# Attention's projections as two 64-row lanes from rows with halves exchanged, and the maxima transposed behind the values

## The chip, the cores and the metric

The program runs on one core of one Trainium2 chip. The metric is the device time of one execution in microseconds (us), the median over runs. TensorE (PE) multiplies matrices from SBUF into PSUM banks, and its weight loads (PEld) are listed apart. VectorE (DVE), ScalarE (ACT) and GpSimd (POOL) work on SBUF and PSUM, and SyncE (SP) starts the DMAs. Each engine takes its instructions in program order.

## The reference

Four layers follow one another on an array x of 2048 rows and 640 columns: spectral, attention, spectral, attention. Each adds its result to x.

```
x = x + A(layernorm(x));  x = x + B(layernorm(x));  x = x + A(layernorm(x));  x = x + B(layernorm(x))
A: y = Cr @ (x @ Wr.T) - Ci @ (x @ Wi.T)            # Fourier mixing over columns, then over rows
B: q, k, v = split(x @ wqkv)                         # 32 heads of 20 columns
   scores = q @ k.T / sqrt(20); a row sees itself and the 255 rows ahead of it
   o = softmax(scores) @ v;  y = o @ wo
```

## The kernel before

Each product of f32 data is made of f16 parts: both factors are split into a high and a low part, and three of the four combinations are added up. A product over 640 columns is thus 15 matmuls of 128 rows each (five pieces of 128 columns, three combinations) into one PSUM bank. Such products in attention are q and k ("qk": 128 columns of weights as the stationary side, 256 rows of x streamed, QB = 256), v (320 columns of weights streamed) and out (320 columns streamed, HD = 320). All matmuls and transposes go through one helper, `tensor` (L116), which also fixes their order on PE to the order in which the code is written.

Attention (`attention`) goes through 8 blocks of 256 rows, and each block takes 32 steps `g`, one for each pair of query tile and heads, 256 steps in a layer and some more for the work that lags behind. A step does, in this order on PE:

- `scores(g)`: four matmuls into tile sp, each on 64 of the array's 128 rows (62 used), two heads side by side. DVE then masks (L1054) and takes the maximum of each row (m, L1058).
- `by_key(g - KEY_LAG)`: six matmuls into tile tp, the same scores turned so that keys lie in rows, again 64-row tiles. ACT makes the softmax weights from them, ptq (L1102), and POOL applies masks. There is one tile tp of two banks, so the next step's tp waits until ACT has read this one.
- every fourth step `values`: 32 f32 matmuls into tile pv, in four column tiles of 32. ACT copies the result to pvs (L1135), and `back` (two steps later) turns it back and divides.
- every fourth step `hand_on`: the maxima of four steps (tile tops) are transposed on PE into a bank of pool p3, and ACT copies them into two rows of the query tile (qs, L1079, `copy_tops`), where by_key's matmuls subtract them. HAND_LAG = 4 puts the transposes at the end of a step, and the two copies come one and two steps later.
- `run_fill`: the projections of the next block, out products of the block before, and turns (transposes of rows for them) fill PE in between. A list `fill` holds them as units that become ready at some step and have a due step. Each step gets a budget of PE time, `rate`, times a factor from the table FILL, which has one number for each of the four steps of a period.

Each unit of a product runs to its end in one of the two banks of pool pf, its result is taken out by ACT (qf L334, v L824) or DVE (x L879), and a turn uses the single bank of pool p3. The copies that take a turn out of PSUM are L952 (DVE) and L954 (ACT). The results q and k go to DRAM and come back as stacks by heads, 160 KB a DMA. `last_out` makes the out products of the last block piece by piece, as heads become ready; L852 adds them to x and SP writes 160 KB each time.

In PSUM lie then: pf two banks, sp two, tp two, pv one, p3 one. SP issues all DMAs (L174).

Of the kernel before, what the change touches and what calls it, by code (L numbers as in the profile page):

```python
# [11 lines left out]
F32 = mybir.dt.float32  # L12
# [17 lines left out]
NST = 5  # L30
EARLY = 4 * ND * P + NST * 2 * QB
# [3 lines left out]
FILL = (1.3, 1.12, 0.28, 1.3)  # L35
# [7 lines left out]
HAND_LAG = 4  # L43
# [7 lines left out]
TURN_ROOM = 1000  # L51
NORM_STEPS = (4, 9)
# [10 lines left out]
def body(ctx: ExitStack, tc: tile.TileContext, x_in, cmat, whid, wqkv, wo, out):  # L63
# [3 lines left out]
    pf_ = ctx.enter_context(tc.tile_pool(name="pf", bufs=1, space=bass.MemoryType.PSUM))  # L67
# [42 lines left out]
    in_turn, latest = [False], [None]  # L110
# [74 lines left out]
    def new_f():  # L185
        return pf_.tile([P, 512], F32, tag="f", name="pf", bufs=2)

# [12 lines left out]
    B11, T2, B21, T3, T1, T4, B22 = range(7)  # L200

    class Hidden:
# [21 lines left out]
        def stage(self, s, pool, new=new_f):  # L224

            w, xt = self.w, self.xt(s)
            if s % 8 < 2:
                zc = new_early()[:, :14 * HD].rearrange("p (m a d) -> p m a d", m=7, a=2)
            else:
                zc = pool.tile([P, 7, 2, HD], F16, tag="zc", name="zc", bufs=4)  # L230
            self.zc[s] = zc
            b11, b12, t1, t2, t3, t4 = (self.zf[:, k] for k in range(6))
            z = None

            def product(c, n):
                nonlocal z
                z = new()
                cs = slice(n * HD, (n + 1) * HD)
                k = 0
                for dt in range(ND):  # L240
                    for l, r in ((0, 0), (0, 1), (1, 0)):
                        self.last = matmul(z[:, :HD], xt[:, l, dt], w[:, r, c, dt, cs],
                                                     start=k == 0, stop=k == 14).ins
                        k += 1
                        yield 136
                z = z[:, :HD]
# [11 lines left out]
            yield from product(0, 0)  # L258
            scaled(zc[:, B11, 0])
            scaled(b11)  # L260
            minus(zc[:, B11, 1], zc[:, B11, 0])
            yield 0
            yield from product(0, 1)
            scaled(b12)
            minus(t1, b11)
            parts(T1, t1)
            yield 0
            yield from product(1, 1)
            scaled(zc[:, B22, 0])
            minus(t2, t1)  # L270
            minus(t3, b12)
            minus(zc[:, B22, 1], zc[:, B22, 0])
            parts(T2, t2)
            parts(T3, t3)
            yield 0
            yield from product(1, 0)
            scaled(zc[:, B21, 0])
            minus(zc[:, B21, 1], zc[:, B21, 0])
            minus(t4, t2)
            parts(T4, t4)  # L280
            yield 0

    def new_stack():
        return new_quad("ks").bitcast(F16).rearrange("p (a b) -> p a b", a=NP)

# [13 lines left out]
    class Projections:  # L299


        def __init__(self):
            n = 3 * ND * D
            big = new_big()
            self.w = [big[:, k * n:(k + 1) * n].rearrange("p (a b) -> p a b", a=ND) for k in range(2)]
            load_behind([(big[:, k * n:(k + 1) * n], bw_d[k].rearrange("p a b -> p (a b)")) for k in range(2)])
            self.rows = {}
            self.turn = 0
            self.stack = {}

        def new_rows(self, b):
            t = new_early()
            n = 2 * ND * P
            x = t[:, :2 * n].rearrange("p (t a b c) -> p t a b c", t=2, a=2, b=ND)
            st = t[:, 2 * n:].rearrange("p (m a t) -> p m a t", m=NST, a=2)
            self.rows[b] = (x, [st[:, k] for k in range(NST)])

        def qk(self, b, w, ct):
            pf = new_f()
            cols = slice(w * D + ct * P, w * D + (ct + 1) * P)  # L320
            xt, stores = self.rows[b]
            k = 0
            for dt in range(ND):
                for l, r in ((0, 0), (0, 1), (1, 0)):
                    matmul(pf[:, :QB], self.w[l][:, dt, cols], xt[:, :, r, dt, :],
                                     start=k == 0, stop=k == 14)
                    k += 1
                    if k < 15:
                        yield 109
            t = stores[self.turn % len(stores)]  # L330
            self.turn += 1
# [6 lines left out]
            yield 109  # L338
# [5 lines left out]
    def spectral(layer, res_src, hidden, first):  # L344
        with ExitStack() as st:
# [6 lines left out]
            sb = pool("sb")  # L352
            pxy = banks("px")
            w = hidden.w
# [210 lines left out]
            def ahead(proj):  # L565
# [3 lines left out]
                for w in (1, 0):  # L569
                    for ct in range(ND):  # L570
                        for _ in proj.qk(0, w, ct):
                            pass
                        yield 1
# [3 lines left out]
            def finish(j, pace):  # L577
# [15 lines left out]
                for k, xs in enumerate(xss):  # L593
                    for m in range(2):
                        transposed(xs, m, proj.rows[j][0][:, k])
                        yield 1
                    finished[0] += 1
# [168 lines left out]
    def attention(layer, proj, dst, final):  # L766
        with ExitStack() as st:
# [6 lines left out]
            sb = pool("sb")  # L774
            if layer == 0:
# [6 lines left out]

            def new_turn():

                return p3.tile([P, 512], F32, tag="f", name="pt") if in_turn[0] else new_f()
# [15 lines left out]
            def proj_qk(b, w, ct):  # L801
                yield from proj.qk(b, w, ct)
# [3 lines left out]
            def proj_v(b, ti, n):  # L806
                j = 2 * b + ti
                if n == 0:
# [4 lines left out]
                pf = new_f()  # L813
                cols = slice(2 * D + n * 320, 2 * D + (n + 1) * 320)
                k = 0
                for dt in range(ND):
                    for l, r in ((0, 0), (0, 1), (1, 0)):
                        matmul(pf[:, :320], proj.rows[b][0][:, ti, l, dt, :], proj.w[r][:, dt, cols],
                                         start=k == 0, stop=k == 14)
                        k += 1  # L820
                        if k < 15:
                            yield 136
# [3 lines left out]
                yield 136  # L826

            def out_turn(i, k):
                if k == 0:
                    X2[i] = keep.tile([P, D], F32, tag="res", name="x3", bufs=4)  # L830
                    load(X2[i], x2_d[i])
                    OT[i] = sb.tile([P, 2, ND, P], F16, tag="ot", name="ot", bufs=2)
                yield from turned(OS[i // 2][:, :, i % 2], k, OT[i])
                done.add((i, k))

            def last_out(i, d0, d1):

                if d0 == 0:
                    x3 = keep.tile([P, D], F32, tag="res", name="x3", bufs=4)
                    load(x3, x2_d[i])  # L840
                    OT[i] = (sb.tile([P, 2, ND, P], F16, tag="ot", name="ot", bufs=2),
                             ps.tile([P, 2, 512], F32, tag="ts"[i % 2 == 0], name="acc"), x3)
                ot, acc, x3 = OT[i]
                for k in range(2):
                    yield from turned(OS[i // 2][:, :, i % 2], k, ot, d0, d1)
                for n in range(2):
                    yield from out_products(ot, acc[:, n], n, d0, d1)
# [7 lines left out]
                if not final:  # L855
                    yield from next_layer(i, x3)

            def out_products(ot, o, n, d0, d1):
                cs = slice(n * 320, (n + 1) * 320)
                for dt in range(d0, d1):  # L860
# [441 lines left out]
```

## Time and profile before

| | |
|---|---|
| time, median of 3 runs | 2274.68 us (2274.08 to 2276.71) |
| the profiled execution: its time, its span, its granted clock | 2273.16 us, 2271.4 us, 0.987 |
| attention's steps, first layer | about 600 to 1152 us of the span |
| attention's steps, second layer | about 1717 to 2240 us of the span |
| DMA | 292.94 MB, mean 129 GB/s, 254 in the busiest of 40 slices |

The span is the time between the first and the last record of the profile, and the profiled execution's own time is 1.8 us longer. In the profile's rows a start and a duration stand first. The duration of a matmul includes its latency, so what a matmul costs in a stream is read from start to start. "Waits" list idle time of an engine and what ended it; "the chain" is the work that ended last, followed back.

### The profile page before, as it was taken

What the parts mean: (1) busy time and instruction counts of PE and PEld (TensorE: products, weight loads), DVE (VectorE), ACT (ScalarE), POOL (GpSimd) and SP (SyncE); (2) the same over time, 40 slices, a digit from 0 to 9 for tenths busy, and PEclk for the clock granted to TensorE, in tenths of its full rate; (3) what the DMA queues carried; (4) which work ended last, traced back from release to release, by engine and by line L of the source; (5) the groups of instructions that cost most, each with busy time, mean ns of one, the idle gap of its engine ahead of it and who ended that gap; (6) DMA issues with size and microseconds to landing.
All of it is one profiled execution on the core that took longest, in us unless ns stands there. A gap on an engine that the chain in (4) does not pass through costs nothing.

```text
span 2271.4 us, 55086 instructions
## 1 busy us (share of the span) xinstructions
PE 2132.5 (94%) x21985; PEld 1498.7 (66%) x21985; DVE 1632.5 (72%) x3577; ACT 1291.8 (57%) x2159; POOL 1387.0 (61%) x1788
## 2 busy tenths in 40 slices
PE   7989889899899999999898999999998999999997
PEld 4757666667666666677555777777676666777664
DVE  7886758866678787886756858585757777777664
ACT  6434455443367777777754443433434777777775
POOL 5775868857355665565445858586674545566443
PEclk9999999999999999999999999999999999999999
DMA  7664646454532322333324536363643323332231
GB/s 247 214 214 136 211 162 213 162 194 165 138 83 68 94 75 72 92 90 86 129 76 142 195 130 207 112 207 137 254 125 97 81 57 83 93 95 56 56 76 36
DMA packets 187605, 292.94 MB, mean 129 GB/s; under 512 B 13908, under 2 KB 120660, under 8 KB 178004
## 3 DMA queue, kind: packets, MB, share of 16 engines
q1 hardware_dynamic: 187348, 289.43, 40.9%
q8 instruction: 172, 2.82, 0.5%
q14 instruction: 85, 0.70, 0.1%
HBM read 202.51 MB, written 86.87 MB: 127 GB/s over the span
## 4 chain that ended last, share of the span: by engine, by line
PE 61%; DVE 14%; issue 5%; POOL 4%; ACT 3%; DMA 2%; SPq 0%; DVEq 0%; POOLq 0%; ACTq 0%
PE pf L116 25%; PE pv L116 8%; PE y L116 8%; PE z L116 5%; PE x L116 5%; PE sp L116 5%; DVE m L1058 3%; DVE sp L1054 3%; PE tp L116 3%; PE pt L116 2%; DVE cc L488 2%; ACT ptq L1102 1%; DMA x<-x2d 1%; DVE lnt L141 1%; PE acc L116 1%
## 5 line engine op out<-in xcount | busy, mean ns | idle before, releaser
L116 PEld LDWEIGHTS <-cc 128*128 128x128 f16 x5376 | 526.7, 98 | 220.6 <-issue 17.6
L1102 ACT ACTIVATE ptq<-tp,shift,alpha 128x768 f32<-128x768 f32 (+2 forms) x512 | 486.7, 951 | 176.1 <-PE tp L116 166.0
L116 PEld LDWEIGHTS <-big 128*128 128x128 f16 x4320 | 410.6, 99 | 148.7 <-issue 34.0
L1058 DVE TENSOR_REDUCE m<-sp 128x2 f32<-128x512 f32 (+1 forms) x512 | 344.9, 674 | 16.7
L1054 DVE COPY_PREDICATED sp<-mask,sp 128x256 f32<-128x256 int32 x448 | 191.0, 426 | 203.0 <-PE sp L116 186.7
L1107 POOL TENSOR_SCALAR_AFFINE_SELECT ptq<-ptq 128x512 f32<-128x512 f32 x224 | 145.4, 649 | 261.2 <-ACT ptq L1102 260.5
L116 PE MATMUL pf<-early,big 128*128 128x256 f16 x2400 | 304.5, 273 | 0.0
L485 ACT ACTIVATE cc<-cs 128x512 f16<-128x512 f32 x256 | 151.6, 623 | 241.3 <-POOL cs L478 119.2
L116 PE MATMUL y<-zc,cc 128*128 128x320 f16 x1728 | 266.3, 301 | 6.4 <-DVE pf L511 6.1
L488 DVE SCALAR_TENSOR_TENSOR cc<-cs,cc 128x512 f16<-128x512 f32 x256 | 252.2, 1000 | 13.2 <-ACT cc L485 12.9
L116 PE MATMUL pf<-big 128*128 128x320 f16 x1680 | 243.7, 304 | 17.2 <-DVE zc L256 8.3
L488 DVE SCALAR_TENSOR_TENSOR cc<-cq,cc 128x512 f16<-128x512 f32 x192 | 192.2, 1002 | 0.1
L1109 POOL TENSOR_SCALAR_AFFINE_SELECT ptq<-ptq 128x512 f32<-128x512 f32 x256 | 164.1, 641 | 43.7 <-ACT ptq L1102 43.7
L116 PE MATMUL pv<-ptq,v 128*32 128x128 f32 (+1 forms) x3840 | 183.8, 331 | 0.0
L116 PE MATMUL z<-zc,cc 128*128 128x320 f16 x1152 | 179.7, 301 | 3.7 <-DVE res L511 3.7
L116 PE MATMUL x<-zc,cc 128*128 128x320 f16 x1152 | 180.2, 301 | 0.0
L116 PE MATMUL sp<-ks,qs 62*128 62x256 f16 (+1 forms) x1792 | 154.3, 249 | 17.2 <-DVE m L1058 15.1
L1079 ACT ACTIVATE qs<-pt 2x512 f16<-2x512 f16 x224 | 131.4, 586 | 47.8 <-PE pt L116 45.2
L116 PE MATMUL pf<-big,early 128*128 128x320 f16 x960 | 157.6, 300 | 0.8 <-DVE x L879 0.8
L116 PE MATMUL tp<-qs,ks 62*128 62x128 f16 x2688 | 150.6, 217 | 4.4 <-ACT ptq L1102 3.4
L116 PE MATMUL pf<-bo,ot 128*128 128x320 f16 x840 | 141.9, 302 | 6.1 <-DVE ot L952 6.1
L116 PEld LDWEIGHTS <-ks 62*128 62x128 f16 x3008 | 116.5, 94 | 43.3 <-DVE m L1058 20.1
(143 smaller groups left out, 3495.6 us busy)
## 6 DMA issues: line engine op xcount, KB each, us to landing
cq<-in_cmat_dram SPq DMA_DIRECT2D x64, 1024.0 KB
accd<-res SPq DMA_DIRECT2D x96, 320.0 KB
res<-accd SPq DMA_DIRECT2D x96, 320.0 KB
x<-x2d SPq DMA_DIRECT2D x64, 320.0 KB
qkd<-early SPq DMA_DIRECT2D x160, 128.0 KB
ks<-qkd SPq DMA_DIRECT2D x108, 160.0 KB
qs<-qkd SPq DMA_DIRECT2D x84, 160.0 KB
x2d<-res SPq DMA_DIRECT2D x32, 320.0 KB
```

The costliest lines, as they stand in the source:

```text
L116: i = getattr(nc.tensor, what)(*args, **kw)
L141: ts(u, g, g, h, op0=OP.mult, op1=OP.mult)
L485: nc.scalar.activation(cc[m][:, 0], f, AF.Copy, scale=C_UP)
L488: nc.vector.scalar_tensor_tensor(cc[m][:, 1], f, C_UP, cc[m][:, 0], op0=OP.mult, op1=OP.subtract)
L1054: nc.vector.copy_predicated(sp[:, :, 2 * P:3 * P], mask[:, None, :].to_broadcast([P, 2, P]), far)
L1058: topped[0] = nc.vector.tensor_reduce(TOP[g // 4][:, g % 4], sp[:, :, c0:3 * P], axis=AX.X, op=OP.max).ins
L1079: nc.scalar.activation(o, handed[n][rs].rearrange("r (i p) t -> r i p t", i=2), AF.Copy)
L1102: nc.scalar.activation(q[:, h:h + 2, a0 + first:a0 + 3], tp[:, :, first * P:3 * P].rearrange("p a (b c) -> p a b c", c=P), AF.Sigmoid, bia ...
L1107: nc.gpsimd.affine_select(out=q[:, :, a0], in_=q[:, :, a0], pattern=[[0, 4], [-1, P]], base=0, channel_multiplier=1, compare_op=OP.is_gt, ...
L1109: ins = nc.gpsimd.affine_select(out=q[:, :, a0 + 2], in_=q[:, :, a0 + 2], pattern=[[0, 4], [1, P]], base=0, channel_multiplier=-1, compare ...
```

## The change

The products qk, v and out become units of class `Product`, each bound to a lane. A lane is half of the array's rows: lane 0 is rows 0 to 63, lane 1 rows 64 to 127. A product is 30 matmuls of 64 rows instead of 15 of 128, and two products, one on each lane, run side by side, each into a bank of its own. The 640 columns are ten chunks of 64. Five of them lie on rows 0 to 63 and five on rows 64 to 127, so each lane needs the other five as well: a second copy of the rows is held with the two halves exchanged, which `swap` makes with two DMAs from SBUF to SBUF. Weights are laid out anew on the host for that. q and v's first half and out's first half are on lane 0, k and the second halves on lane 1. If a lane has nothing ready, the other's matmul goes alone.

Three banks (two of pool pf, one of p3) rotate among the two lanes and the turns: `spare` gives the one used longest ago, and a new product or turn starts when that bank has been free for CLEAR = 600 of the planner's ns. A product whose rows are swapped is ready SWAP_STEPS = 2 steps after the DMA's issue.

`hand_on` moves from the end of a step to right behind `values` in the same step, and its transposes go into the half of the bank pv that values leaves free. ACT's two copies qs follow at once, and the copy pvs comes behind them. FILL changes.

In all SP issues 1118 DMAs instead of 974, PE does 24385 matmuls instead of 20065.

```diff
-NST = 5
-EARLY = 4 * ND * P + NST * 2 * QB
+NST = 3
+EARLY = 8 * ND * P
-FILL = (1.3, 1.12, 0.28, 1.3)
+FILL = (0.95, 1.45, 0.1, 1.5)
-HAND_LAG = 4
+HAND_LAG = 5
+TURN_PAIRS = 8
+CLEAR = 600
+SWAP_STEPS = 2
+    PARTS = (0, 0), (0, 1), (1, 0)
+    def swap(o, x):
+        for h in range(2):
+            load(o[half(h)], x[half(1 - h)])
+        def operands(self, b, ct, h, k):
+            c, (l, r) = k // 3, PARTS[k % 3]
+            w = self.w[l][half(h), c, ct * P:(ct + 1) * P]
+            return w, self.rows[b][c % 2 != h][half(h), :, r, c // 2, :]
...
             def rows_turn(b, xs, t, k):
                 yield from turned(xs, k, proj.rows[b][0][:, t])
-                done.add(("rows", b, t, k))
+                if k:
+                    swap(proj.rows[b][1][:, t], proj.rows[b][0][:, t])
+                    done["rows", b, t] = now[0] + SWAP_STEPS
...
+            class Product(Unit):
+                def begin(self):
+                    self.bank = spare()
+                    self.pf = take(self.bank, "pf")
+                    lanes[self.lane] = self
+                def step(self):
+                    matmul(self.pf[:, :self.cols], *self.operands(self.done), start=self.done == 0, stop=self.done == 29)
+                    self.done += 1
...
+            def advance(kinds=()):
+                for h in range(2):
+                    if unit[0] is None and lanes[h] is None:
+                        u, v = next_product(h, kinds), next_single()
+                        if v is not None and (u is None or v.due < u.due):
+                            fill.remove(v)
+                            unit[0] = v
+                        elif u is not None and (clear(spare()) or lanes[1 - h] is None):
+                            fill.remove(u)
+                            u.begin()
...
+                live = [u for u in lanes if u is not None]
+                for u in live:
+                    u.step()
+                charge(max([u.ns for u in live] or [0]))
...
             def hand_on(n):
-                hp = new_turn().bitcast(F16)[:, :4 * P].rearrange("p (a b) -> p a b", a=4)
+                hp = new_pv()[:, 2:].bitcast(F16).rearrange("p a (c b) -> p (a c) b", c=2)
...
-                for pi in range(2):
-                    n, m = divmod(g - HAND_LAG - 1 - pi, 4)
-                    if m == 0 and 0 <= n < NG // 4:
-                        copy_tops(n, pi)
                 slow_step()
                 n, m = divmod(g - VALUE_LAG, 4)
                 if m == 0 and 0 <= n < NG // 4:
                     for part in range(2):
                         values(n, part)
+                n, m = divmod(g - HAND_LAG, 4)
+                if m == 0 and 0 <= n < NG // 4:
+                    hand_on(n)
+                    for pi in range(2):
+                        copy_tops(n, pi)
+                n, m = divmod(g - VALUE_LAG, 4)
+                if m == 0 and 0 <= n < NG // 4:
+                    copy_values(n)
...
                 run_fill(ns)
-                n, m = divmod(g - HAND_LAG, 4)
-                if m == 0 and 0 <= n < NG // 4:
-                    hand_on(n)
```

On PE, a step with values in the second attention layer, before: the last of by_key's matmuls (tp), the values (pv from ptq and v), and a fill product of 128 rows (pf from the weights big and the rows early). The maxima have been transposed one step earlier, ahead of that step's scores.

```order
L116 MATMUL tp_29033<-qs_27561,ks_27280 128x128
L116 MATMUL pv_23547<-ptq_28813,v_27731 32x256 x4
L116 MATMUL pv_23547<-ptq_28813,v_26454 32x128 x4
L116 MATMUL pv_23547<-ptq_28813,v_26638 32x256 x4
L116 MATMUL pv_23547<-ptq_28813,v_27940 32x128 x4
L116 LDWEIGHTS early_27068
L116 MATMUL pf_29018<-big_21824,early_27068 128x320
```

The fill comes right behind the values there. The same engine at such a step with the change:

```order
L118 MATMUL tp_33104<-qs_30926,ks_31002 128x128
L118 MATMUL pv_25815<-ptq_32849,v_31428 32x256 x4
L118 MATMUL pv_25815<-ptq_32849,v_29789 32x128 x4
L118 MATMUL pv_25815<-ptq_32849,v_30036 32x256 x4
L118 MATMUL pv_25815<-ptq_32849,v_31708 32x128 x4
L118 LDWEIGHTS tops0_74
L118 MATMUL pv_25815<-idh_66,tops0_74 66x128
```

The transposes of the maxima (from tops) now stand behind the values, into the same tile pv, four of them. The end of that step on PE with the change, where names ending in 63 and 64 are the high and low part of wo, 32994 and 33042 the banks of the two lanes, and sp is the next step's scores:

```order
L118 LDWEIGHTS tops0_74
L118 MATMUL pv_25815<-idh_66,tops0_74 66x128
L118 LDWEIGHTS ot_32861
L118 MATMUL pf_32994<-bo0_63,ot_32861 128x320
L118 LDWEIGHTS ot_32861
L118 MATMUL pf_33042<-bo1_64,ot_32861 128x320
L118 LDWEIGHTS qs_32488
L118 MATMUL sp_33138<-ks_31002,qs_32488 128x128
```

One pair of 64-row matmuls is all the fill that is left in this step, and the next scores come behind it without a change of the tile's height. On ACT before, around a pair of copies of the maxima (qs) in the second layer:

```order
L334 ACTIVATE qf<-pf 128x256
L1102 ACTIVATE ptq<-tp,shift,alpha 128x2x384
L334 ACTIVATE qf<-pf 128x256
L1079 ACTIVATE qs<-pt 2x2x2x128 x2
L1102 ACTIVATE ptq<-tp,shift,alpha 128x2x384
L1135 ACTIVATE pvs<-pv 128x256
L1102 ACTIVATE ptq<-tp,shift,alpha 128x2x384
```

Between qs and pvs stands one ptq. On ACT with the change:

```order
L981 ACTIVATE ot<-pt 128x640
L1185 ACTIVATE ptq<-tp,shift,alpha 128x2x384
L1162 ACTIVATE qs<-pv 2x2x2x128 x2
L1224 ACTIVATE pvs<-pv 128x256
L1185 ACTIVATE ptq<-tp,shift,alpha 128x2x384 x2
L981 ACTIVATE xto<-pt 128x640
L1185 ACTIVATE ptq<-tp,shift,alpha 128x2x384 x2
```

The two copies qs and the copy pvs now stand together, and the ptq of the following step is behind all three.

More of the change, by code (lines that the diff above doesn't have):

```diff
@@ L222, in fetch, with operands, leave @@
             load(self.xt(s).rearrange("p a b c -> p (a b c)"), self.xt_src[s])
[L224 to L231, printed above, removed]
-            b11, b12, t1, t2, t3, t4 = (self.zf[:, k] for k in range(6))
[L233 to L246, printed above, removed]
+        def operands(self, s, c, n, k):
+            dt, (l, r) = k // 3, PARTS[k % 3]
+            return self.xt(s)[:, l, dt], self.w[:, r, c, dt, n * HD:(n + 1) * HD]
+        def leave(self, s, m, pool, z):
+            if m == 0:
+                if s % 8 < 2:
+                    zc = new_early()[:, :14 * HD].rearrange("p (m a d) -> p m a d", m=7, a=2)
+                else:
+                    zc = pool.tile([P, 7, 2, HD], F16, tag="zc", name="zc", bufs=4)
+                self.zc[s] = zc
+            zc = self.zc[s]
+            b11, b12, t1, t2, t3, t4 = (self.zf[:, k] for k in range(6))
+            z = z[:, :HD]
             def parts(m, f):
@@ L568, in ahead @@
                 yield 1
[L569 to L573, printed above, removed]
+                for ct in range(ND):
+                    proj.both(0, ct, new_f, new_store)
+                    yield 1
+                    yield 1
             finished = [0]
```

351 lines of the change are left out of this document (198 added, 153 removed).

## The prediction

> **What bounds the kernel now.** I read the totals first, then the chain, then attention's stretches, and last the rows of single steps. The page's totals:
>
> ```profile
> span 2271.4 us, 55086 instructions
> PE 2132.5 (94%) x21985; PEld 1498.7 (66%) x21985; DVE 1632.5 (72%) x3577; ACT 1291.8 (57%) x2159; POOL 1387.0 (61%) x1788
> ...
> GB/s 247 214 214 136 211 162 213 162 194 165 138 83 68 94 75 72 92 90 86 129 76 142 195 130 207 112 207 137 254 125 97 81 57 83 93 95 56 56 76 36
> ...
> PE 61%; DVE 14%; issue 5%; POOL 4%; ACT 3%; DMA 2%; SPq 0%; DVEq 0%; POOLq 0%; ACTq 0%
> ```
>
> PE is busy 94% and holds 61% of the chain; ACT has room on average. The change touches attention, so I cut out its first and last stretches and one from the middle (columns: window, length, then busy time and instructions of PE, PEld, DVE, ACT, POOL, the clock, the DMA share, GB/s):
>
> ```profile
> 600.00:650.00 50.00, 44.28 (x453) 29.18 (x452) 42.98 (x103) 33.76 (x61) 23.47 (x50) 1.00 0.37 109
> 1100.00:1150.00 50.00, 42.71 (x577) 28.21 (x575) 34.95 (x84) 37.59 (x56) 22.06 (x38) 0.90 0.31 113
> 1700.00:1750.00 50.00, 45.89 (x410) 30.99 (x408) 33.75 (x84) 19.27 (x37) 17.43 (x38) 1.00 0.41 99
> 1950.00:2000.00 50.00, 49.70 (x683) 34.49 (x682) 34.43 (x84) 37.83 (x55) 27.62 (x55) 1.00 0.35 88
> 2200.00:2250.00 50.00, 41.70 (x622) 26.82 (x615) 31.76 (x78) 39.16 (x53) 22.00 (x42) 1.00 0.03 12
> ```
>
> In the middle PE is full (49.70 of 50), so every ns taken from PE there, or put on it, is a ns of time. At both ends of each layer it idles 5.72, 7.29, 4.11 and 8.30 us, 25.4 together. Four steps of the middle on PE (start, duration of the group, matmuls):
>
> ```profile
> 2011.48 0.39 PE L116 MATMUL pt<-idh,tops 128*66 128x128 f16 x4
> 2011.80 0.34 PE L116 MATMUL sp<-ks,qs 62*128 62x256 f16 x4
> 2011.98 0.33 PE L116 MATMUL tp<-qs,ks 62*128 62x128 f16 x6
> 2012.24 1.51 PE L116 MATMUL pv<-ptq,v 128*32 128x256 f32 x32
> 2013.68 0.50 PE L116 MATMUL pf<-early,big 128*128 128x256 f16 x3
> 2014.11 0.34 PE L116 MATMUL sp<-ks,qs 62*128 62x128 f16 x4
> 2014.29 0.33 PE L116 MATMUL tp<-qs,ks 62*128 62x128 f16 x6
> 2014.55 1.92 PE L116 MATMUL pf<-early,big 128*128 128x256 f16 x16
> 2016.40 0.34 PE L116 MATMUL sp<-ks,qs 62*128 62x128 f16 x4
> ```
>
> Prices in a stream are read from start to start. Sixteen pf take 1.85 us, three take 0.43; thirteen more cost 1.42, that is 109 ns each, and sixteen by that are 1.744. The remaining 106 ns are the price of one change of the tile's height (a full tile followed by half tiles, or the other way). The same rest stands in pt to sp: 0.32 for four transposes of about 56 ns, rest 96. Six tp on half tiles take 0.26, less such a change 0.16: two run at once, 54 ns a pair of 128 columns, so pairs of half tiles ran at full rate here.
>
> ACT in the same steps, PE's waits, and pieces of the chain:
>
> ```profile
> 2011.90 1.19 ACT L1079 ACTIVATE qs<-pt 2x512 f16<-2x512 f16 x2 [0.48 <-PE pt L116]
> 2013.12 0.99 ACT L1102 ACTIVATE ptq<-tp,shift,alpha 128x768 f32<-128x768 f32 x1
> 2014.63 0.37 ACT L1135 ACTIVATE pvs<-pv 128x256 f32<-128x256 f32 x1
> 2014.90 0.38 ACT L334 ACTIVATE qf<-pf 128x256 f32<-128x256 f32 x1
> ```
>
> ```profile
> PE sp L116 <- DVE m L1058: 23.8, 43, 1.1
> PE pt L116 <- ACT ot L954: 8.4, 15, 2.3
> PE pt L116 <- DVE xto L952: 5.5, 9, 1.2
> PE tp L116 <- ACT ptq L1102: 4.1, 14, 0.5
> PE pt L116 <- DVE early L952: 2.3, 5, 1.1
> PE pt L116 <- ACT xto L954: 1.6, 3, 1.2
> PE pt L116 <- ACT early L954: 1.5, 6, 0.4
> PE pt L116 <- DVE ot L952: 1.4, 4, 0.5
> ```
>
> ```profile
> 2240.73 1.00 ACT ptq L1102
> 2241.77 0.36 PE tp L116 x6
> ...
> 2267.64 0.55 DVE x L852
> ```
>
> (Waits: total us, times, longest.) PE waits only 4.1 us for ptq now, and the six rows with pt and a turn's copy, 20.7 us, are turns or maxima that wait for the one bank p3. From ptq's start to the next tp are 1.04 us.
>
> **The change, part by part.** Counts are mine, along the written order of both programs; durations are the rows'.
>
> 1. *Fewer changes of height: −33.9 us.* Scores and tp use half tiles; with fill on half tiles too, fill between them needs no change. PE's order has 1160 changes before and 840 after (in the two attentions 1119 and 770): 320 × 106 ns. PE is the full engine where they go.
>
> 2. *Pairs that are not full: +14.4 us.* A full pair costs what one 128-row matmul cost. Rows with 320 columns:
>
> ```profile
> 2193.09 0.45 PE L116 MATMUL pf<-big,early 128*128 128x320 f16 x2
> 2196.08 1.39 PE L116 MATMUL pf<-big,early 128*128 128x320 f16 x9
> ```
>
> Seven more cost 0.94, 134 ns each. The order has 2260 pairs of 256, 1754 of 320, 212 of one with the other, and 188 matmuls alone (68 of 256, 120 of 320). One alone wastes half its time: (68 × 0.109 + 120 × 0.134)/2 = 11.7; an unequal pair wastes half the difference, 212 × 0.0125 = 2.7. No row shows a lone one's neighbour overlapping it, so I take the whole.
>
> 3. *Banks: −12 us.* The maxima go into pv's free half and need no turn's bank, and turns take the one of three banks that has been free longest. Of the 20.7 us the whole may go or nothing; near the layers' ends copies follow turns as closely as now, so I take somewhat over half.
>
> The Trainium skill, TensorEngine Tiling (Array Packing), Restrictions and Gotchas, says that row tiling raises the pressure on PSUM, since row tiles at work together must write to different banks. By that rule two of the three banks are always held by lanes, and the third has only just been emptied; this term would be 0 and the sum 12 us higher. The trace of before has no two lanes, so it can't decide it.
>
> 4. *The maxima behind the values: +37.8 us.* This is the term that decides. Follow ACT from the start of tp in a step with values, with the rows above. The values start 0.26 later (2011.98 to 2012.24) and end at 0.26 + 1.44 = 1.70; there the transposes stand now. Their copies start 0.42 after them (2011.48 to 2011.90): 2.12. Two copies take 1.22 (2011.90 to 2013.12): 3.34. The copy pvs is next in ACT's order, 0.27 (2014.63 to 2014.90): 3.61. Only then comes ptq of the next step, whose tp has long been there, and from its start to the next tp are 1.04: the tp of two steps on cannot start before 4.65 us. Before, the maxima stood ahead of the scores, the copies were 1.22 of 2.31 us between two tp (2011.98 to 2014.29), and pvs lay behind ptq; this just fits, as the 4.1 us of waits say. What PE has to do from tp to the tp of two steps on, by the new order at the prices above: values, transposes, scores and tp twice and fill of 0.1 and 1.5 parts, 4.25 us on average in 88 periods of four steps in the layers' middles. In 76 of these it is under 4.65, and the shortages add up to 37.8 us. Queued behind the waiting tp on PE are that step's fill and the next scores; PE can't overtake, so the time is lost. Bounds: 0, if ACT's order doesn't hold ptq back; 44, if each of the 88 periods loses 0.5, the longest wait for ptq seen. The upper is nearer, since the terms are rows.
>
> 5. *The same in the 34 thin periods of the layers' ends: +8 us.* There the shortage is counted as 44.1 us, but PE idles 25.4 us there already, mostly for DVE (23.8 us for m). The bounds are 0 and 44.1 − 25.4 = 18.7; I take a value just under the middle.
>
> 6. *Swaps: +10 us.* 144 DMAs more in SP's queue. In the steady part a swapped product comes at least two steps later, 2.7 us of fill at the least, mostly over 4.5. The cover fails in the layer's tail (last out pieces) and ahead of the first products of q and k. No row shows such a copy; the nearest are the last write of 160 KB, over 3.2 us after its add (2267.64 + 0.55 to the span's end at 2271.4), and a load of 320 KB at a stage's start:
>
> ```profile
> 1616.46 6.29 DMA x<-x2d
> ```
>
> I take 3 us in each of two tails and 2 in each of two starts. Bounds: 0, and four times 6.29, 25. The stacks of q and k, whose products now end together, make 12 loads (1.97 MB) in eight steps of about 2 us; at the 254 GB/s of the busiest slice that takes 7.7 of 16 us, so I take nothing.
>
> Extra issues on POOL and DVE: none; the evictions stay as many. Sum: −33.9 + 14.4 − 12 + 37.8 + 8 + 10 = +24.3. The profiled execution took 2273.16, which gives 2297.5; the median of runs is 1.5 above that execution, so I forecast 2299.
>
> **The rivals.**
>
> *Faster: the chain over ACT doesn't bind.* It decides at one point: if PE's work from a values step's tp to the tp two steps on is 4.65 us or more (or ACT needs only 4.2), terms 4 and 5 go, and −33.9 + 14.4 − 12 + 10 = −21.5 leaves 2251.7, 2253 as a median. For it: the fill behind the values is the larger part now, and 12 of 88 periods reach it; my 4.25 needs each price right to a tenth. Against: the copies, pvs and ptq stand in a row in the order, and each has its row.
>
> *No change that can be measured.* With half of 4 and 5 (22.9 in place of 45.8) the sum is +1.4, a median near 2276. For it: other waits of PE in the same periods (m, 23.8 us) may take place beside ptq's.
>
> *Slower by more: PE can't issue pairs that fast.* In the full stretch PE did 683 matmuls in 50 us, 73 ns each. If that were a floor, a pair would take 146 ns in place of 109 and 134: 2260 × 37 + 1966 × 12 = 107 us. Fill then covers ACT's chain: 2273.2 − 21.5 + 107 is 2359, 2360 as a median. Against it: the six tp at 27 ns each. But they are a burst of six.
>
> The Trainium skill, TensorE: Matmul & The Clock Gate, section Back-to-back issue gap, gives about 81 ns per matmul for a sustained stream of weight loads and matmuls at 128 columns. By that a pair needs 162 ns, and 2260 × 53 + 1966 × 28 = 175 us would come on top. The trace's 109 ns at 256 columns doesn't contradict it, and the six tp do, for so short a stretch.
>
> **How the numbers follow.** About 0.2% (4.5 us) is what a measurement of this kernel can tell from no change: faster is below 2270, slower above 2279. Chances: slower by the ACT chain 0.50, faster 0.34, no change 0.11, issue bound 0.05. The last counts as slower too: 0.34, 0.11, 0.55. The likeliest case has its own range: half widths of 10 for the chain, 9.5 for the thin periods, 10 for banks and 12 for swaps, added as independent, make 21: 2279 to 2320. The faster case spans 2253 − 8.7 (all of the banks) − 10 (no swap waits) to 2253 + 12 + 15. The whole range reaches from 2246, which leaves a quarter of the faster case below, to 2320, which leaves out the issue bound and the top of the likeliest: about 0.2 outside.
>
> **What the profile after would show.** Term 1: in sp, tp, fill, sp no 0.1 us gaps. Term 2: thirty pairs of 256 in 3.3 us, more if issue binds. Term 3: rows of pt waiting for turns' copies under 10 us in all. Term 4: a row of PE tp waiting for ACT ptq with some 30 to 45 us in 80 to 100 times, about 0.4 each; if it stays under 10, the faster case holds. Term 6: PE waiting for a DMA into ot or early, in the tail and ahead of the steps. The prediction is wrong above all if the fill of the step behind the values is longer on the chip than I count, or ACT finishes the copies sooner out of pv's bank than out of p3's.

## The result, and the profile after

The changed kernel takes 2465.12 us (median; 2462.14 to 2466.57), the kernel before 2275.69 beside it: ratio 1.0825, interval 1.0802 to 1.0848. It is slower by 190 us, where 24 were forecast and 2246 to 2320 us was the range.

The page's totals after:

```profile
span 2464.8 us, 63987 instructions
PE 2188.2 (89%) x26305; PEld 1558.0 (63%) x26305; DVE 1649.8 (67%) x3577; ACT 1291.4 (52%) x2159; POOL 1384.8 (56%) x1788
...
PE 47%; DMA 11%; DVE 10%; ACT 8%; POOL 6%; issue 5%; SPq 2%; POOLq 0%; DVEq 0%; ACTq 0%
```

PE has gone from 94% to 89%, and DMA from 2% to 11% of the chain: PE waits for data. The two attention stretches, of the kernel before and then of the changed one (columns as in the prediction's windows):

```profile
600.70:1152.00 551.30, 521.12 (x6904) 360.79 (x6903) 435.09 (x1120) 405.29 (x613) 302.46 (x546) 0.99 0.32 87
1717.10:2240.40 523.30, 501.32 (x6729) 347.09 (x6728) 384.91 (x952) 382.34 (x574) 280.70 (x529) 1.00 0.28 72
```

```profile
611.00:1233.00 622.00, 533.79 (x8744) 383.62 (x8745) 436.09 (x1118) 405.25 (x614) 301.56 (x546) 0.95 0.35 91
1806.00:2425.00 619.00, 520.06 (x8609) 372.61 (x8609) 391.68 (x952) 381.68 (x575) 280.16 (x534) 0.93 0.31 75
```

They grew from 1075 to 1241 us, 166 of the 190, and the granted clock in them (the share of TensorE's full clock that the chip granted) fell from 0.99 and 1.00 to 0.95 and 0.93. The busy time of DVE, ACT and POOL changed by under 1% (DVE 820 to 828 us in the two stretches together). PE's longest waits after (total us, times, longest):

```profile
PE tp L118 <- ACT ptq L1185: 38.5, 78, 1.7
PE pf L118 <- DMA ot<-ot: 28.8, 3, 13.5
PE sp L118 <- DMA ks<-qkd: 28.2, 10, 5.0
PE sp L118 <- DVE m L1141: 28.1, 50, 1.2
PE pf L118 <- ACT qf L343: 16.5, 20, 1.7
...
PE sp L118 <- DMA x<-x2d: 10.7, 2, 5.8
PE sp L118 <- DMA early<-early: 10.0, 4, 4.6
...
PE pf L118 <- ACT v L851: 3.5, 4, 1.2
```

The wait for ptq is the forecast one. The waits for DMAs (ot, ks, early and what the list names x<-x2d) are new: before, all waits of PE for a DMA came to 0.4 us. The list names the transfer that landed last; the scores (sp) read only the stacks ks and qs, so sp's rows with early, ot, x<-x2d or x3d<-x, 31 us in all, are most likely waits for a stack too. Rows around a values step of the second layer:

```profile
2101.75 0.33 PE L118 MATMUL tp<-qs,ks 62*128 62x128 f16 x6
2102.01 1.51 PE L118 MATMUL pv<-ptq,v 128*32 128x256 f32 x32
2103.45 0.41 PE L118 MATMUL pv<-idh,tops 128*66 128x128 f16 x4
...
2104.11 0.33 PE L118 MATMUL tp<-qs,ks 62*128 62x128 f16 x6
...
2106.41 0.34 PE L118 MATMUL tp<-qs,ks 62*128 62x128 f16 x6 [0.55 <-ACT ptq L1185]
```

From the values step's tp to the tp two steps on are 2106.41 − 2101.75 = 4.66 us, with 0.55 of waiting at its end; the prediction had worked out 4.65. And a run of full pairs in the first layer:

```profile
956.46 0.33 PE L118 MATMUL tp<-qs,ks 62*128 62x128 f16 x6
956.63 2.02 PE L118 MATMUL pf<-early,big 64*128 64x256 f16 x34
```

Seventeen pairs end 2.02 us after their start; less the last one's own 0.27 (the page's mean for such a matmul is 270 ns) that is 16 steps of 109 ns. Pairs run at full rate, and there is no change of height ahead of them (956.46 to 956.63 is three pairs of tp).

The next table says where the 166 us of the attention stretches are. I laid the order of PE's matmuls, at the prediction's prices, beside their starts in the trace. "Order at full rate" is what the matmuls would take one behind the other. Each excess over it is put to the matmul ahead of which it stands, or, where it is under 0.5 us and the clock is at half, to the clock ("half clock"). The split is an estimate from these prices. In us, both layers:

| kernel | measured | order at full rate | ahead of sp | of fill (pf) | of tp | of turns, maxima and values | half clock | rest |
|---|---|---|---|---|---|---|---|---|
| before | 1074.2 | 977.2 | 33.8 | −0.8 | 9.6 | 42.6 | 5.4 | 6.4 |
| changed | 1240.3 | 945.0 | 111.5 | 62.8 | 49.2 | 21.2 | 42.3 | 8.3 |

The order became 32 us shorter there, so PE was given less to do, and each of four kinds of loss (ahead of sp, of fill, of tp, and the half clock) grew by more than that. The trace's own clock records agree with the last: in these stretches PE worked 12 us at a granted clock of 0.50 before and 93 us after, and half of such time is lost.

### The profile page after: what moved, and what is told of

Same layout as the page of the kernel before. It is cut to its first block, busy times and chain, and to the rows that moved or that the text cites. A ratio compares the mean times of both kernels' runs of the same rounds, so it can differ in the third digit from the quotient of the medians.

```text
span 2464.8 us, 63987 instructions
## 1 busy us (share of the span) xinstructions
PE 2188.2 (89%) x26305; PEld 1558.0 (63%) x26305; DVE 1649.8 (67%) x3577; ACT 1291.4 (52%) x2159; POOL 1384.8 (56%) x1788
## 4 chain that ended last, share of the span: by engine, by line
PE 47%; DMA 11%; DVE 10%; ACT 8%; POOL 6%; issue 5%; SPq 2%; POOLq 0%; DVEq 0%; ACTq 0%
PE pf L118 17%; PE pv L118 8%; PE y L118 7%; PE x L118 5%; PE z L118 5%; DMA qkd<-qkst 3%; DMA ks<-qkd 3%; ACT qs L1162 3%; ACT ptq L1185 3%; PE tp L118 2%; SPq L176 2%; PE sp L118 2%; DVE m L1141 2%; PE pt L118 2%; DVE cc L507 2%
## 5 line engine op out<-in xcount | busy, mean ns | idle before, releaser
L118 PEld LDWEIGHTS <-cc 128*128 128x128 f16 x5376 | 527.9, 99 | 229.4 <-issue 23.7
L118 PEld LDWEIGHTS <-big 64*128 64x128 f16 (+1 forms) x6720 | 432.9, 96 | 166.6 <-issue 52.2
L118 PE MATMUL pf<-early,big 64*128 64x256 f16 x4800 | 331.3, 270 | 17.5 <-ACT qf L343 14.2
L507 DVE SCALAR_TENSOR_TENSOR cc<-cs,cc 128x512 f16<-128x512 f32 x256 | 253.4, 1005 | 12.8 <-ACT cc L504 12.7
L118 PE MATMUL sp<-ks,qs 62*128 62x256 f16 (+1 forms) x1792 | 170.3, 250 | 82.7 <-DMA ks<-qkd 28.2
L118 PE MATMUL pf<-big 128*128 128x320 f16 x1560 | 227.1, 306 | 17.0 <-DVE early L248 8.0
L118 PE MATMUL pf<-bo,ot 64*128 64x320 f16 x1680 | 188.8, 304 | 34.4 <-DMA ot<-ot 28.8
L118 PE MATMUL pf<-big,early 64*128 64x320 f16 x1920 | 205.1, 308 | 2.6 <-ACT v L851 1.5
L118 PE MATMUL tp<-qs,ks 62*128 62x128 f16 x2688 | 164.9, 222 | 37.8 <-ACT ptq L1185 37.2
L118 PE MATMUL pv<-ptq,v 128*32 128x128 f32 (+1 forms) x3840 | 193.1, 343 | 0.0
L118 PEld LDWEIGHTS <-ks 62*128 62x128 f16 x3008 | 132.2, 96 | 92.1 <-issue 65.3
L1162 ACT ACTIVATE qs<-pv 2x512 f16<-2x512 f16 x224 | 131.4, 587 | 81.5 <-PE pv L118 80.0
```

The lines of the kernel that those rows point to most:

```text
L118: i = getattr(nc.tensor, what)(*args, **kw)
L507: nc.vector.scalar_tensor_tensor(cc[m][:, 1], f, C_UP, cc[m][:, 0], op0=OP.mult, op1=OP.subtract)
L1162: nc.scalar.activation(o, handed[n][rs].rearrange("r (i p) t -> r i p t", i=2), AF.Copy)
```

## Experiments

Each kernel was timed against the kernel before on the same chip, whose medians there were 2273.6 to 2275.1 us. None came under the kernel before.

**Data that comes late.** On SP around a block's end in the changed kernel (start, duration, what is issued), then the end of the chain there, and stretches before, behind and after the gap:

```profile
888.24 3.36 SPq L176 DMA_DIRECT2D qs<-qkd  x6
891.70 1.11 SPq L176 DMA_DIRECT2D qkd<-qkst  x1
892.86 0.88 SPq L176 DMA_DIRECT2D ks<-onesd  x2
898.04 3.52 SPq L176 DMA_DIRECT2D ks<-qkd  x6
901.67 1.64 SPq L176 DMA_DIRECT2D early<-early  x2
```

```profile
902.72 6.02 DMA early<-early
908.74 0.08 issue
908.82 0.26 PE sp L118
```

```profile
903.50:908.70 5.20, 0.68 (x9) 0.36 (x7) 0.66 (x4) 1.07 (x2) 0.75 (x2) 0.83 1.06 221
908.80:913.80 5.00, 4.98 (x52) 3.08 (x56) 3.68 (x10) 1.98 (x2) 1.23 (x2) 0.50 0.63 168
914.00:919.00 5.00, 4.69 (x83) 3.25 (x73) 2.86 (x9) 4.47 (x8) 2.62 (x3) 1.00 0.32 118
```

The last product of k is stored at 891.70; behind it in SP's queue, after two small loads, the six loads of the stack wait for that store to land and issue at 898.04; the swap stands behind them and issues at 901.67; the scores start at 908.82, 17 us after the store. The chain names the swap, since it landed last, but the first scores need the stack alone. Before, at the same block's end, the loads were issued like this, and PE had no such wait:

```profile
835.43 3.24 SPq L174 DMA_DIRECT2D ks<-qkd  x6
...
855.34 2.90 SPq L174 DMA_DIRECT2D qs<-qkd  x6
```

The two stacks stood 20 us apart and only the second came near the end. Now q's loads are issued at 888.24 and k's at 898.04, 10 us apart: k and q end together at step 24 of 32, which leaves about 16 us for both. Behind the gap PE runs 5 us at a granted clock of 0.50 with hardly a break, and gets 52 matmuls done; in the next 5 us, at 1.00, it does 83. The longest wait for ot is of the same kind:

```profile
1136.73 6.01 DMA qkd<-qkst
...
1147.67 8.08 DMA ot<-ot
...
1155.80 1.24 PE pf L118 x7
```

*e1_noswap*: `swap` does nothing, products read `rows[b][0]` and `OT[i][:, 0]`.

> The changed kernel without the swaps: every product reads the first copy of its rows only, so half of its chunks multiply the wrong rows. No swap DMA is issued or waited for. Theory 1 (data comes late: swaps and stack loads stand one behind the other in SP's queue): the waits of PE for DMAs into ot and early (46 us) go, the stack loads start earlier, and the clock that is lost behind those waits comes back: about 2375 us (2350 to 2400). Rival (pairs of half-tile matmuls are slow in themselves, waits only show it): 2450 to 2470 us.

2413.26 us, 1.061 times the kernel before (interval 1.0587 to 1.0634; so in all that follow): 52 us back. It is neither answer: PE's waits for ot and early went, but the stacks stayed late.

```profile
PE sp L118 <- DMA ks<-qkd: 40.0, 14, 5.0
PE tp L118 <- ACT ptq L1184: 39.9, 80, 1.7
```

*s1_unread*: swaps issued as they are, read by nobody.

> The changed kernel with all swaps issued as they are, but read by nobody: products read the first copy only, so half of their chunks multiply the wrong rows. With swaps it took 2465 us, without them 2413. Theory 1a (the 52 us are PE's waits for the swapped copy): 2410 to 2425 us. Theory 1b (they are the place that 144 DMAs take in the queue and on the DMA engines, ahead of the stack loads): 2445 to 2470 us.

2431.27 us, 1.0695 (1.0676 to 1.0714), between the two answers: both theories hold a part. Of the 52 us, 34 go when nobody reads the copies, so they are waits for them; the other 18 go only with the DMAs themselves, their place in queue and engines.

*e2_qk20*, where QK_SLOT is the step of a block's 32 by which q and k of the next block are due:

```diff
-QK_SLOT = 24
+QK_SLOT = 20
```

> The changed kernel with the products of q and k due at step 20 of a block's 32 (QK_SLOT 24 to 20), four steps or about 9 us earlier. Theory 1: the gaps of about 5 us ahead of the first scores of a block (14 of them, waiting for stores, stack loads and swaps in one queue) go, with 3 us of half clock behind each: 2360 to 2400 us. Rival (the products' work itself is what makes the block late): the wait only moves into the earlier steps, 2440 to 2475 us.

2490.04 us, 1.0952 (1.092 to 1.0983): slower by 25, over both answers, so the theory as I put it fell. The wait for ks has left the list, but now the swaps of the out products stand in SP's queue behind the stacks' stores and loads (SP first, then PE's wait):

```profile
800.30 1.04 SPq L176 DMA_DIRECT2D qkd<-qkst  x1
...
806.00 3.21 SPq L176 DMA_DIRECT2D ks<-qkd  x6
809.32 1.47 SPq L176 DMA_DIRECT2D ot<-ot  x2
```

```profile
PE pf L118 <- DMA ot<-ot: 100.6, 15, 16.0
```

*e5_pool*: `nc.gpsimd.dma_start` in `swap` in place of SP's.

> The changed kernel with the swap DMAs issued by POOL in place of SP; nothing else differs. Theory 1 (a swap waits in SP's queue behind stores and stack loads that wait themselves): PE's waits for DMAs into ot and early, 46 us, fall under 15, and the stack loads, which no longer stand behind swaps, come earlier: 2400 to 2430 us, about what leaving the swaps out gave. Rival (the landing itself, 6 to 8 us beside the stack loads, is what is waited for, whatever the queue): 2445 to 2475 us.

2455.02 us, 1.0793 (1.0771 to 1.0814): the rival's time, though not for its reason. Fill's wait for ot fell from 28.8 to 3.5 us, as the theory had it, but the stacks came no earlier. All of sp's waits for DMAs, under whatever name, were 58.9 us in the changed kernel and are 72.4 here, so what was saved ahead of fill was partly waited for ahead of sp:

```profile
PE sp L118 <- DMA ks<-qkd: 58.9, 18, 5.8
...
PE sp L118 <- DMA x<-x2d: 13.5, 3, 5.0
```

*e6_qk20_pool*: both edits.

> The changed kernel with q and k due at step 20 and the swap DMAs issued by POOL. Theory 1: with the stacks in time (their wait was gone at step 20) and the swaps out of SP's queue, PE's waits for DMAs in attention fall from about 90 us under 25, and half of the lost clock comes back: 2340 to 2390 us. Rival (earlier stack loads hold up the swaps on the DMA engines, not in the queue): ot is still waited for, 2430 us or more.

2399.97 us, 1.0539 (1.0505 to 1.0572), 65 us under the changed kernel, though 10 over the range that I gave. Each edit alone gave −10 (POOL) and +25 (step 20): the two waits stood one behind the other. PE's waits for DMAs fell from some 90 to 39 us, not under 25:

```profile
PE pf L118 <- DMA ot<-ot: 18.1, 10, 7.6
...
PE acc L118 <- DMA ot<-ot: 10.7, 3, 5.9
PE sp L118 <- DMA ks<-qkd: 9.4, 4, 3.3
```

*g2_swap4*: SWAP_STEPS = 4 in f1_fill (below, 2414.56 us).

> The kernel f1_fill with SWAP_STEPS = 4 in place of 2: a product whose rows are swapped becomes ready two steps later. Theory 1: landing takes 6 to 8 us beside other loads, so four steps cover it: the waits for ot (28 us in e6) fall under 10, 15 to 30 us faster than f1_fill with the clock. Rival (the later products then press on their due steps): within 5 us of f1_fill.

2421.51 us, 1.0654 (1.0621 to 1.0687): not faster, and at 7 us over f1_fill near the rival. Fill's wait for ot went from f1_fill's 12.7 us to 1.7, that for ptq rose from 21.4 to 27.3, and that for m from 56.5 to 66.2.

**A wait and the clock.** *e7_b28*: the kernel before with `QK_SLOT = 28`.

> The kernel before with q and k due at step 28 in place of 24, so that their stacks come late at the blocks' ends; full tiles, no swaps. Theory 3 (a wait of 3 us or more of PE costs itself and some 3 us more at half clock behind it, whatever the products' form): 12 to 14 gaps of 4 to 7 us ahead of first scores and the granted clock down to about 0.965: 2340 to 2400 us. Rival (late stacks are hidden by the older kernel's order, the clock follows something else): 2270 to 2300 us.

2315.63 us, 1.0182 (1.0163 to 1.0202), between the two answers. The gaps came, smaller than I had put them:

```profile
PE sp L116 <- DMA qs<-qkd: 32.8, 11, 4.3
```

```profile
core 0: 2312.6 us, clock 0.980
```

33 us of waits cost 42, a quarter on top. By the clock records PE worked 38 us of attention at half clock here, against 12 in the kernel before, which is 13 us of full clock. So the lanes are not needed for it.

**The moved maxima.** *e4_bmax*: the kernel before with `hand_on`, both `copy_tops` and then the copy pvs right behind `values`, in pv's free half; nothing else.

> The kernel before with one part of the change alone: maxima transposed behind the values into pv's free half, both copies qs and then pvs on ACT; products on full tiles, FILL as before. Theory 2: PE waits 30 to 50 us for ptq, partly paid by turns that no longer share their bank with maxima (up to -12): 2295 to 2330 us. Rival (the chain costs nothing without the lanes): 2262 to 2282 us.

2310.9 us, 1.0163 (1.0141 to 1.0185): +37 us, as theory 2 says. The wait for ptq rose by 26 us and that for m by 9:

```profile
PE sp L116 <- DVE m L1058: 33.0, 61, 1.6
PE tp L116 <- ACT ptq L1102: 30.2, 62, 1.4
```

*e3_oldmax*: the changed kernel with `hand_on` at the end of a step, the copies one and two steps later, the old FILL.

> The changed kernel with the maxima transposed at the end of a step and copied one and two steps later, as before (HAND_LAG 4, the old FILL), still in pv's free half. Theory 2 (ACT's copies qs, qs, pvs in a row hold back ptq): PE's wait for ptq falls from 38.5 to under 8 us, with the clock 2465 becomes about 2425 us (2410 to 2440). Rival (the wait moves on to other copies or to DMAs): 2450 to 2475 us.

2453.06 us, 1.0793 (1.0761 to 1.0825), −12: the rival. The wait for ptq fell to 8.7 us and another took its place, since maxima and values share the tile pv:

```profile
PE pv L118 <- ACT qs L1162: 25.9, 70, 2.7
```

*e8_dve*: second copy qs and copy pvs by `nc.vector.tensor_copy`.

> The changed kernel with the second copy qs and the copy pvs on DVE in place of ACT. Theory 2: ACT's chain ahead of ptq shortens from 4.65 to about 3.8 us, under the 4.25 that PE has to do; PE's wait for ptq falls from 38.5 under 12 us: 2415 to 2440 us. Rival (the waits move to DVE's maxima m, which stand behind these copies): 2455 to 2475 us.

2475.75 us, 1.0887 (1.0865 to 1.0908): the rival, slower by 11. ptq's wait fell to 4.9 us, and m came late, since the copies stand in DVE's order too:

```profile
PE sp L118 <- DVE m L1141: 86.1, 139, 1.9
```

*f1_fill*: e6 with FILL (0.75, 1.15, 0.1, 2.0).

> The kernel with q and k due at step 20 and swaps issued by POOL (e6), with FILL changed from (0.95, 1.45, 0.1, 1.5) to (0.75, 1.15, 0.1, 2.0): more of a period's fill stands behind the values. Theory 2: PE then has some 4.8 us from a values step's tp to the tp two steps on, over ACT's 4.65; the wait for ptq falls from 38.7 under 15 us: 2355 to 2380 us against e6's 2400. Rival (the thinner steps then wait for DVE's maxima m): 2390 to 2410 us.

2414.56 us, 1.0602 (1.0571 to 1.0632), 15 over e6 and 5 over the rival's range. ptq's wait fell from 38.7 to 21.4 us, m's rose from 33.0 to 56.5, which is the rival's reason.

*g1_pvs*: e6 with the copy pvs behind the next ptq.

> The kernel e6 with one edit: the copy pvs is issued behind the next step's ptq in ACT's order. Theory 2: the chain ahead of ptq shortens by 0.27 us, from 4.65 to 4.38, in some 75 periods: the wait for ptq falls from 38.7 to about 20 us, 2375 to 2388 us against 2400. Rival (something else than the three copies holds ptq back): 2393 to 2407 us.

2395.69 us, 1.0536 (1.0514 to 1.0558). ptq's wait fell to 22.2 us as expected, the time by 4, within the two intervals of each other: inconclusive for the time. Its attention stretches are 1162 us, e6's 1172.

**Two lanes, three banks.** *f2_clear*: f1_fill with CLEAR = 1500.

> The kernel f1_fill with CLEAR = 1500 in place of 600: a lane begins a new product only when its bank has been free 1.5 us of planned time, so the two lanes no longer end together. Theory 4 (both lanes end at once, three banks are too few, and the next products wait for the copies qf and v): the waits for qf and v fall from 17 to under 8 us, and matmuls that go alone cost some 5 back: 5 to 15 us faster than f1_fill. Rival (going alone costs as much as waiting): within 4 us of f1_fill, or slower.

2456.46 us, 1.0801 (1.0784 to 1.0817), 42 over f1_fill. The wait for qf fell only from 14.4 to 9.2 us. PE's order at full rate in attention became 20 us longer (matmuls that go alone, 948 to 968), and ot was waited for 47.5 us, up from 12.7. The rival, and dearer than it; since the wait for ot rose as well, this run doesn't price the banks alone.

**The lanes alone.** *h3_b20*: the kernel before with `QK_SLOT = 20`.

> The kernel before with q and k due at step 20 in place of 24: a control for the due step alone. Theory 1 (its stacks were in time already): 2268 to 2290 us. Rival (the earlier due step costs by itself, as thinner steps at the blocks' ends wait for m): 2295 us or more.

2295.01 us, 1.0098 (1.0074 to 1.0122): +21, at the edge of the rival: the earlier due step costs by itself.

*h2_noswap*: the changed kernel without swaps, due step 20, maxima at the end of a step in one of the rotating banks with both copies at once, FILL as before.

> The same without any swap: products read the first copy only, so half of their chunks multiply the wrong rows; q and k due at step 20. What is left of the change is pairs on three banks. If pairs are as fast as their order says (16 us less PE work than before in attention), only the waits for qf and v (about 20 us) and their clock stand against it: 2270 to 2310 us. Rival (pairs themselves are slow): 2340 us or more.

2313.92 us, 1.0175 (1.0155 to 1.0195), near the first answer. Against h3_b20, with the same due step, it is 19 us more: pairs aren't slow, but don't gain either.

*s3_pairs24*: the same at due step 24.

> h2_noswap with the due step of q and k back at 24: pairs on three banks, no swaps (half of the products' chunks multiply the wrong rows), maxima as before. The due step cost 21 us in the old kernel. If q's and k's stacks come in time at 24 when no swaps stand between them: 2280 to 2300 us. If both stacks behind the last products are late by themselves (6 us to store, 3 us of issues, 6 us to land): 2330 to 2370 us.

2389.24 us, 1.0511 (1.0493 to 1.0529), 19 over the second answer: 75 us over h2_noswap, where the old kernel gained 21 by the same step. The due step is the only difference, so without any swap q and k that end together are late:

```profile
PE sp L118 <- DMA ks<-qkd: 35.1, 13, 5.1
...
PE sp L118 <- DMA x<-x2d: 14.9, 3, 6.2
```

*h1_lanes*: h2_noswap with swaps, issued by POOL.

> The lanes without the move of the maxima: e6 (q and k due at step 20, swaps issued by POOL) with the maxima transposed at the end of a step into one of the three rotating banks, both copies at once, pvs one step later, and FILL as before. If the moved maxima and the late data were the whole loss, ptq's wait falls from 39 under 10 us and m's to about 25: 2330 to 2360 us. Rival (the lanes bring waits of their own: both end at once and wait for qf and v, turns and out products for a swap, and each wait costs clock): 2375 to 2410 us.

2378.57 us, 1.0461 (1.0429 to 1.0493): the rival, at the lower end of its range. *s2_unread*: the same with nobody reading the swapped copies.

> h1_lanes with its swaps issued by POOL but read by nobody, products reading the first copy only (half of their chunks wrong). With the swaps read it took 2379 us, without any 2314. Theory 1a (waits for the copy): 2314 to 2330 us. Theory 1b (traffic and queues): 2360 to 2380 us.

2350.54 us, 1.0356 (1.0303 to 1.0409), again between the two. Of the swaps' 65 us here, 37 are traffic and queues, 28 waits. The four kernels in attention, split as in the table above:

| attention, us | measured | order | ahead of sp | of fill | of tp | half clock |
|---|---|---|---|---|---|---|
| h3_b20 | 1097.3 | 978.6 | 38.7 | 8.6 | 8.6 | 13.6 |
| h2_noswap | 1105.0 | 961.4 | 55.7 | 5.5 | 18.4 | 12.3 |
| s2_unread | 1137.5 | 961.4 | 72.9 | 8.5 | 18.1 | 23.7 |
| h1_lanes | 1152.1 | 961.4 | 77.3 | 13.0 | 17.6 | 30.1 |

So a way from one kernel to the other at due step 24, each step a run: pairs with both stacks at a block's end +115 (s3_pairs24), the moved maxima +24 (e1_noswap), the swaps' DMAs +18 (s1_unread), the waits for their copies +34 (the changed kernel), 191 in all. The sizes depend on the order in which they are added, as e2, e5 and e6 show.

## Why the prediction was wrong

The direction was right, for a reason that accounts for a fifth of it; that the rest pushed the same way is luck.

- Terms 1 and 2, −33.9 and +14.4, sum −19.5. PE's order at full rate is 32 us shorter in attention and 12 longer outside it, 20 in all: right, by the trace's matmuls at the prediction's prices, and pairs ran at 109 ns. The rival that PE can't issue pairs that fast is dead. So is the estimate of 162 ns a pair, worked out from the 81 ns a matmul at 128 columns of the Trainium skill (TensorE: Matmul & The Clock Gate, Back-to-back issue gap): the trace has 109 for seventeen pairs of 256 columns in a row with their weight loads. That the sum by that estimate came near the measured one is chance.
- Term 4, +37.8: the wait for ptq rose by 34 us, the chain is 4.66 us long, and the part alone cost 37 (e4_bmax). The mechanism is right, and so is the size of the wait; what it is worth in time depends on what else PE waits for, 24 us on the way above and 12 when it alone is taken back (e3_oldmax). Term 5, +8: m's row rose by 4.
- Term 3, −12: the waits of turns, maxima and values together fell by 21 us, but the products now wait 20 us for qf and v. That two lanes which end together find one free bank is argued from the program; f2_clear, which keeps them apart, cut the wait for qf only from 14.4 to 9.2 us. The row of after bears out what the Trainium skill says (TensorEngine Tiling (Array Packing), Restrictions and Gotchas) about pressure on PSUM: the term is about 0, as the prediction worked out beside it.
- Term 6 failed, and with the half clock behind its waits it is most of the error. It had +10 us for swaps and nothing for the stacks. The rows of after with a DMA add up to some 90 us, and by the runs the swaps cost 52 us (e1_noswap) and the stacks at step 24 cost 75 (s3_pairs24 over h2_noswap). Two steps of it were wrong. A swap was priced by its own landing, with cover counted in steps, and not by SP's queue, where it stands behind a store's landing (6.0 us) and six loads (3.5 us) that wait for it, and takes 6 to 8 us itself beside the stack loads. And the stacks were held covered because 7.7 us of bytes fit into 16: but store, wait, issues and loads come one after another, 17 us by the rows above. I had seen that q and k end together, and had costed it by bandwidth.
- A term was missing: the clock. In attention work at half clock cost 37 us more than before (42.3 − 5.4), besides the waits themselves, and the prediction priced every wait at its length alone. The trace of before held the price: its clock of 0.987 stands for 60 us at half clock, and most of these stretches follow waits of 2 to 6 us.

## What to carry to other kernels

Price a transfer from the event that frees its source to the event that needs it, along the queue it is issued in: what stands ahead of it there, and what that waits for, before its bytes. Two producers made to finish together make their stores and loads finish together, at the end of the slack that one of them had alone. On an engine that is full, a wait of a few us can cost more than its length (here 33 us of them cost 42), so many small gaps are worth more than the work saved between them; and where several waits stand in a row, removing one shows the next, so a single undo prices none of them.

## What the runs showed of the hardware

The granted clock has two values in these traces, 1.00 and 0.50. Each wait of PE of 2.7 us or more, in the kernel before and in the changed one, has half clock within some 5 us of its start, often while the wait still lasts; of those of 2.0 to 2.6 us some have it and some have not. A few stretches of half clock, such as the one at 1107.5 us before, follow no wait as long as 1 us; in the 3.4 us ahead of that one PE was busy 57%. A stretch lasts 3.41 us or a small multiple of it (the records of the changed kernel show 3.41, 6.83, 10.24, 13.65 and 17.07). In all they are 236 us in the changed kernel and 60 before. PE worked in 153 and 46 us of them, so they cost about 76 and 23 us of full clock; the rest lies in waits, where a slow clock costs nothing. The length agrees with the Trainium skill, TensorE: Matmul & The Clock Gate, What's actually happening, which has windows of about 3.4 us of idling that throttle and of activity that release; the waits of 2.0 us that were followed by half clock here are shorter than such a window. Half clock came with full tiles as with half tiles (e7_b28).

Half tiles had shown full rate in bursts of six before; now seventeen pairs of 256 columns kept 109 ns a pair. Two copies of 160 KB from SBUF to SBUF over 64 partitions, beside the stack loads, took 6.0 and 8.1 us to land.
